# Batch 0's softmax with the maximum as exponential bias, and the preparation of w_in moved off GpSimd

## The chip, the cores and the metric

One core of one Trainium2 chip runs the whole program. The metric is device time in microseconds of one execution, as the median over runs; lower is better.

## What is computed

Three layers follow one another. Inputs are B=4 batches, H=8 heads, S=576 positions, head size 64 (so 2304 tokens of 512 features).

```python
scores = scale * q @ k.T                      # per batch and head
# heads 0-3: key at most 31 behind the query; heads 4-7: key behind, same position mod 32
scores = where(mask, scores, -1e9); scores -= scores.max(-1)
attn = exp(scores); attn /= attn.sum(-1) + 1e-9
x = (attn @ v), tokens by 512
h = x @ w_in                                  # 512 -> 1024, w_in is float64
sm = softmax(h); solu = h * sm; ln = layernorm(solu) * g_ln
x = ln @ w_out                                # 1024 -> 512, w_out is float64
logits = x @ w_gate + modality_bias[modality_id]; e = argmax(logits)
out = gate * (relu(x @ w1[e]) @ w2[e])        # 8 experts
```

## The kernel before

**Stages.** Attention runs in units. A unit is one group of query tiles of one head of a head pair: three tiles of 96 queries by 128 keys for the local heads, four tiles of 72 by 72 for the strided heads. A head pair has 4 units, a batch has 4 pairs, so 16 units: in batch 0 the two strided pairs come first (8 strided units), then the two local pairs (8 local units). `scores` (L310 to L350) makes a unit's matmuls (L326, TensorE to PSUM), adds the mask and takes the row maximum in one VectorE instruction for each tile (L333), and then forms the exponentials in one of two ways, chosen for each batch and head kind by the string `SHIFT_ON`. With "P" or "D", GpSimd or VectorE subtracts the maximum from all tiles of the unit in one instruction (L339), ScalarE takes one exponential over the unit (L342), and `normalise` sums it on VectorE (L357). With "0", VectorE makes the scaled negative maximum (L345, four numbers wide at most), ScalarE takes one exponential for each tile with it as bias and gives the row sum itself (L348, each followed by a read of the accumulator), and L357 is not issued. Before, batch 3 alone has "0". In both ways `normalise` then adds 1e-9 (L358), takes the reciprocal (L359) and multiplies, on GpSimd in most batches (L365). TensorE transposes the result (L127), ScalarE copies it out of PSUM (L376), TensorE multiplies by v (L385), and ScalarE and VectorE split the result into a high and a low part (L397, L398). Units overlap: a unit's transposes and its product with v come two units after its scores (`LAG = 2`).

**w_in.** The matrix multiplies work on float32 in a high and a low part. w_in comes as float64, in 8 pieces of 128 by 512, at fixed places among batch 0's attention steps (`W_IN_AT`). For a piece, `f64_piece` (L200) loads the raw words with SyncE's DMA queue (L203; three buffers, so a load waits for the last reader of the piece three before), scales the upper word (ScalarE L209 or GpSimd L211, by `MAG_ON`), puts in the sign, and ors in the low bits on VectorE (L220). By `SIGN_ON` the sign takes either one GpSimd multiplication by zero (L213) and one VectorE instruction (L214), or two VectorE instructions (L217, L218). `prep_w_in` then casts the high part on ScalarE (L228) and subtracts it for the low part on GpSimd (L229). The first 8 letters of `MAG_ON` and `SIGN_ON` are w_in's, the last 8 are w_out's, whose pieces follow in the same way (L231).

**Order.** The program text interleaves the stages step by step; the framework's scheduler orders the instructions of each engine from dependencies and from a simulated timeline. Each engine then runs its own list in order and waits on semaphores. The second layer (tile by tile of 128 tokens, matmuls L477 and L533) starts when batch 0's units are done; the attention of batches 1 to 3 and the preparation of w_out are spread between its steps by a written list (`TAKES`, `W_OUT_AT`). The experts come last.

Of the kernel before, what the change touches and what calls it, by code (L numbers as in the profile page):

```python
# [9 lines left out]
F32 = mybir.dt.float32  # L10
# [4 lines left out]
ALU = mybir.AluOpType  # L15
# [13 lines left out]
def tile_attention_moe_moe2(  # L29
# [15 lines left out]
    nc = tc.nc  # L45
# [23 lines left out]
    STAGES = "ATPV"  # L69
    PAIRS = [[2, 3, 0, 1]] + [[0, 1, 2, 3]] * (B - 1)  # L70
    NORM_ON = "PPPDPPPP"
    SHIFT_ON = "DPPPPP00"
    MAG_ON = "APAAPAAAPPPAAPPA"
    SIGN_ON = "PDDDDDPPDDDDDDDP"
    LOW_ON = "DPDDPDDD"
    W_IN_AT = [3, 5, 8, 26, 35, 39, 52, 66]
    W_OUT_AT = [1, 1, 2, 3, 3, 3, 4, 6]
# [17 lines left out]
    winH = cst.tile([P, KD, FF], F32R, name="winH")  # L95
    winL = cst.tile([P, KD, FF], F32R, name="winL")
# [104 lines left out]
    def f64_piece(src, tm, tw, by_act, sgn="D"):  # L201
        raw = rawp.tile([P, 512, 2], I32, name="raw")
        nc.sync.dma_start(raw, src)  # L203
        hi, lo = raw[:, :, 1], raw[:, :, 0]
        mag = mp.tile([P, 512], F32, name="mag", tag=tm)
        w = mp.tile([P, 512], F32, name="wf", tag=tw)
        wi = w.bitcast(I32)
        if by_act:
            nc.scalar.activation(mag, hi.bitcast(F32), AF.Copy, scale=REBIAS)  # L209
        else:  # L210
            nc.gpsimd.tensor_tensor(mag, hi.bitcast(F32), rebias.to_broadcast([P, 512]), ALU.mult)  # L211
        if sgn == "P":
            nc.gpsimd.tensor_tensor(hi.bitcast(F32), hi.bitcast(F32), zeros.to_broadcast([P, 512]), ALU.mult)  # L213
            nc.vector.scalar_tensor_tensor(  # L214
                wi, mag.bitcast(I32), 3, hi, ALU.logical_shift_left, ALU.bitwise_or)
        else:
            nc.vector.tensor_scalar(wi, mag.bitcast(I32), 3, None, ALU.logical_shift_left)  # L217
            nc.vector.scalar_tensor_tensor(  # L218
                wi, hi, -2147483648, wi, ALU.bitwise_and, ALU.bitwise_or)
        nc.vector.scalar_tensor_tensor(  # L220
            wi, lo, 29, wi, ALU.logical_shift_right, ALU.bitwise_or)
        return w

    def prep_w_in(i):
        c, hf = divmod(i, 2)
        cs = slice(hf * 512, hf * 512 + 512)
        w = f64_piece(w_in32[:, c, cs], "e", "so", MAG_ON[i] == "A", SIGN_ON[i])
        nc.scalar.copy(winH[:, c, cs], w)  # L228
        nc.gpsimd.tensor_tensor(winL[:, c, cs], w, winH[:, c, cs].bitcast(F32), ALU.subtract)  # L229

    def prep_w_out(f):  # L231
        w = f64_piece(w_out32[:, f], "nH", "yt", MAG_ON[8 + f] == "A", SIGN_ON[8 + f])
        g = gln[:, f:f + 1]
        dst = ((slice(0, HALF), slice(0, HALF)), (slice(HALF, DM), slice(YA, YA + HALF)))
        pool = LOW_ON[f] == "P"
        if pool:
            nc.scalar.activation(w, w, AF.Copy, scale=g)
            g = 1.0
        for s_, d_ in dst:
            nc.scalar.activation(woH[:, f, d_], w[:, s_], AF.Copy, scale=g)  # L240
        for s_, d_ in dst:
            if pool:
                nc.gpsimd.tensor_tensor(woL[:, f, d_], w[:, s_], woH[:, f, d_].bitcast(F32), ALU.subtract)
            else:
                nc.vector.scalar_tensor_tensor(
                    woL[:, f, d_], w[:, s_], g, woH[:, f, d_].bitcast(F32), ALU.mult, ALU.subtract)
        return f, w, g
# [64 lines left out]
    def scores(b, hp, tiles, j, qT, kT):  # L312
# [18 lines left out]
        for i, t in enumerate(tiles):  # L331
# [3 lines left out]
                mx[:nq, i:i + 1])  # L335
        xb = SHIFT_ON[2 * b + (not local)]
        if xb != "0":
# [294 lines left out]
    for i, at_ in enumerate(W_IN_AT):  # L632
        take(at_)
        prep_w_in(i)
# [623 lines left out]
```

## Time and profile before

| | |
|---|---|
| median of 3 runs | 667.8 us (667.05 to 668.77) |
| the profiled execution | 673.7 us, of which its span 672.0 us |
| TensorE busy (matmul) | 614.2 us, 91% of the span |
| VectorE busy | 373.6 us, 56% |
| ScalarE busy | 317.2 us, 47% |
| GpSimd busy | 190.9 us, 28% |

PE is TensorE, PEld its weight loads, DVE VectorE, ACT ScalarE, POOL GpSimd, SP SyncE. A group is all instructions of one line, engine, operation and shape; a wait is idle time of an engine just before an instruction, with what ended it. An engine's busy time includes time in which one of its instructions had started and stood still. The granted clock is a share of TensorE's full 2.4 GHz, so 0.5 is its lower level, 1.2 GHz.

### The profile page before, as it was taken

Reading aid. Unit: us, or ns where it says so; the run is one execution under the profiler, and the core shown is the slowest. Engines: PE = TensorE matmul, PEld = TensorE weight load, DVE = VectorE, ACT = ScalarE, POOL = GpSimd, SP = SyncE. Lnnn points to the kernel's source line nnn. Section 1 sums busy time; section 2 is a strip of 40 time slices with the busy share of each in tenths; the row PEclk is TensorE's granted clock in tenths of the full one; section 3 lists DMA queues with packets and bytes.
Section 4 is the critical chain, followed back from the end, with each engine's and each line's share of the span. In section 5 each row is a group of like instructions: output and inputs, shape, how many; then the busy total and the mean of one; then the engine's idle time right before and its main releaser. Section 6 shows DMA issues by size and latency. Waiting matters only on the chain. (4 is left out here: it accounts for less than half of the span.)

```text
span 672.0 us, 12841 instructions
## 1 busy us (share of the span) xinstructions
PE 614.2 (91%) x4536; PEld 552.3 (82%) x4536; DVE 373.6 (56%) x1367; ACT 317.2 (47%) x723; POOL 190.9 (28%) x243
## 2 busy tenths in 40 slices
PE   5648798999999999998999999999899898999993
PEld 4546687899998989887988999889788787898892
DVE  2999688867776765566569663224346452211120
ACT  3556666746765567778537442223435343221220
POOL 4876344411343234121100422320120302112011
PEclk9555697999999999999999999999899999999997
DMA  8656322121311221111034020253527362112010
GB/s 217 150 152 166 93 72 81 36 66 56 97 52 54 69 74 42 35 34 35 18 131 150 32 90 25 65 177 121 195 82 249 100 213 93 32 64 63 17 48 23
DMA packets 54774, 60.00 MB, mean 89 GB/s; under 512 B 39313, under 2 KB 39313, under 8 KB 54675
## 3 DMA queue, kind: packets, MB, share of 16 engines
q1 hardware_dynamic: 47810, 42.52, 22.2%
q0 software_dynamic: 4272, 11.57, 5.5%
q10 hardware_dynamic: 2592, 4.72, 1.9%
q8 instruction: 47, 0.77, 0.5%
q14 instruction: 53, 0.43, 0.2%
HBM read 49.05 MB, written 10.26 MB: 88 GB/s over the span
## 5 line engine op out<-in xcount | busy, mean ns | idle before, releaser
L845 PE MATMUL py<-w2H,winL 128*128 128x512 f32 x288 | 92.0, 395 | 0.0
L885 PE MATMUL pf<-xTH,w1H 128*128 128x256 f32 x288 | 82.5, 287 | 3.7 <-DVE yo L984 3.7
L885 PE MATMUL pf<-xTL,w1H 128*128 128x256 f32 x288 | 81.5, 283 | 0.3 <-DVE xTL L824 0.3
L885 PE MATMUL pf<-xTH,w1L 128*128 128x256 f32 x288 | 81.4, 283 | 0.0
L892 DVE SCALAR_TENSOR_TENSOR winL<-pf,winL 128x512 fp32r<-128x512 f32 x36 | 24.9, 692 | 95.7 <-ACT winL L891 95.6
L326 PE MATMUL S<-kz,qT 128*72 128x72 f32 (+1 forms) x448 | 60.1, 283 | 17.5 <-DVE mx L333 8.9
L326 PEld LDWEIGHTS S<-kz,qT 128*72 128x72 f32 (+1 forms) x448 | 51.6, 179 | 22.4 <-ACT kz L310 10.5
L365 POOL TENSOR_TENSOR ex<-ex,rd 96x384 f32<-96x384 f32 (+1 forms) x56 | 45.3, 811 | 76.2 <-DVE rd L359 58.3
L891 ACT ACTIVATE winL<-pf 128x512 fp32r<-128x512 f32 x36 | 21.6, 599 | 88.0 <-PE pf L885 87.3
L845 PEld LDWEIGHTS py<-w2H,winL 128*128 128x128 f32 x288 | 53.4, 188 | 10.5
L885 PEld LDWEIGHTS pf<-xTH,w1H 128*128 128x128 f32 x288 | 56.2, 195 | 5.6 <-issue 2.5
L477 PE MATMUL ph<-winH,xTH 128*128 128x512 f32 x144 | 59.9, 416 | 0.1
L477 PE MATMUL ph<-winL,xTH 128*128 128x512 f32 x144 | 57.8, 402 | 0.0
L477 PE MATMUL ph<-winH,xTL 128*128 128x512 f32 x144 | 57.4, 404 | 0.0
L885 PEld LDWEIGHTS pf<-xTL,w1H 128*128 128x128 f32 x288 | 56.2, 195 | 0.8 <-DVE xTL L824 0.5
L885 PEld LDWEIGHTS pf<-xTH,w1L 128*128 128x128 f32 x288 | 56.2, 195 | 0.0
L851 POOL DMA_INDIRECT out_dram<-yo,idx x14 | 14.1, 1007 | 144.3 <-ACT yo L850 121.4
L339 POOL TENSOR_TENSOR ex<-ex,mx 72x288 f32<-72x288 f32 (+1 forms) x40 | 31.3, 784 | 76.7 <-DVE mx L333 42.3
L533 PE MATMUL pa<-woH,nL 128*128 128x264 f32 x144 | 42.8, 297 | 0.0
L533 PE MATMUL pa<-woH,nH 128*128 128x264 f32 x144 | 41.8, 290 | 0.3 <-ACT nH L522 0.3
L533 PE MATMUL pb<-woH,nL 128*128 128x256 f32 x144 | 41.4, 287 | 0.0
L533 PE MATMUL pa<-woL,nH 128*128 128x264 f32 x144 | 41.0, 285 | 0.0
(244 smaller groups left out, 1637.0 us busy)
## 6 DMA issues: line engine op xcount, KB each, us to landing
raw<-in_moe_w_dram SPq DMA_DIRECT2D x36, 512.0 KB
y_d<-yt ACTq DMA_DIRECT2D x18, 256.0 KB
raw<-in_moe_w_in_dram SPq DMA_DIRECT2D x8, 512.0 KB
raw<-in_moe_w_out_dram SPq DMA_DIRECT2D x8, 512.0 KB
vn<-in_v_dram SPq DMA_DIRECT2D x16, 160.0 KB
qn<-in_q_dram SPq DMA_DIRECT2D x8, 288.0 KB
kn<-in_k_dram SPq DMA_DIRECT2D x8, 288.0 KB
vn<-in_v_dram SPq DMA_DIRECT2D x8, 288.0 KB
```

The costliest lines, as they stand in the source:

```text
L326: nc.tensor.matmul(sp_[:nq, i, :nk], qT[:, q0:q0 + nq], kT[:, half, k0:k0 + nk], start=True, stop=True)
L339: eng.tensor_tensor(ex[:nq, :nt, :nk], ex[:nq, :nt, :nk], mx[:nq, :nt].unsqueeze(2).to_broadcast([nq, nt, nk]), ALU.subtract)
L365: nc.gpsimd.tensor_tensor(ex[:nq, :nt, :nk], ex[:nq, :nt, :nk], rd[:nq, :nt].unsqueeze(2).to_broadcast([nq, nt, nk]), ALU.mult)
L477: nc.tensor.matmul(ph, a[:, c, ts_], w[:, c, cs], start=n == 0, stop=n == 3 * KD - 1)
L533: nc.tensor.matmul(p, a[:, f], w[:, f, cols], start=n == 0, stop=n == 3 * KF - 1)
L845: nc.tensor.matmul(p, a[:, f, s], x, start=n == 0, stop=n == 3 * KF - 1)
L851: nc.gpsimd.indirect_dma_start(out=out[:, :], out_offset=indirect(idx[:, col, 2:3].bitcast(U32)), in_=o, in_offset=None, bounds_check=NT - ...
L885: mm = nc.tensor.matmul(p[:, u], a[:, c, fs], x[:, c], start=n == 0, stop=n == 3 * KD - 1)
L891: last[0] = (nc.scalar.activation(hH[:, f2s], p, AF.Relu), nc.vector.scalar_tensor_tensor(hL[:, f2s], p, 0.0, hH[:, f2s].bitcast(F32), ALU ...
L892: nc.vector.scalar_tensor_tensor(hL[:, f2s], p, 0.0, hH[:, f2s].bitcast(F32), ALU.max, ALU.subtract))
```

## The change

Batch 0's two letters of `SHIFT_ON` become "0" (they were VectorE for the local heads and GpSimd for the strided ones). All of w_in's scalings go to ScalarE (pieces 1 and 4 were on GpSimd), all its sign steps to VectorE's two instructions (pieces 0, 6 and 7 used GpSimd), and all 8 subtractions for the low part to VectorE. w_out's letters stay.

```diff
-    SHIFT_ON = "DPPPPP00"
-    MAG_ON = "APAAPAAAPPPAAPPA"
-    SIGN_ON = "PDDDDDPPDDDDDDDP"
+    SHIFT_ON = "00PPPP00"
+    MAG_ON = "AAAAAAAAPPPAAPPA"
+    SIGN_ON = "DDDDDDDDDDDDDDDP"
...
         nc.scalar.copy(winH[:, c, cs], w)
-        nc.gpsimd.tensor_tensor(winL[:, c, cs], w, winH[:, c, cs].bitcast(F32), ALU.subtract)
+        nc.vector.tensor_tensor(winL[:, c, cs], w, winH[:, c, cs].bitcast(F32), ALU.subtract)
```

## Rows read from the trace of the kernel before

**Rows 1.** Busy time by engine in stretches: span, PE, PEld, DVE, ACT, POOL, clock, DMA share, GB/s.

```profile
13.00:74.00 61.00, 36.88 (x258) 30.68 (x260) 56.88 (x185) 35.43 (x71) 42.66 (x45) 0.58 0.61 156
74.00:135.00 61.00, 56.57 (x371) 48.98 (x368) 47.71 (x170) 39.35 (x94) 27.27 (x32) 0.86 0.24 64
135.00:480.00 345.00, 336.85 (x2722) 307.07 (x2720) 210.05 (x919) 185.38 (x459) 81.91 (x107) 1.00 0.25 76
```

**Rows 2.** Groups of VectorE, 0 to 75 us: count | busy us, mean ns | idle before.

```profile
L218 DVE SCALAR_TENSOR_TENSOR wf<-raw,wf 128x512 int32<-128x512 int32 x7 | 7.7, 1107 | 0.1
L214 DVE SCALAR_TENSOR_TENSOR wf<-mag,raw 128x512 int32<-128x512 int32 x3 | 7.2, 2387 | 3.0 <-POOL raw L213 3.0
L339 DVE TENSOR_TENSOR ex<-ex,mx 96x384 f32<-96x384 f32 x8 | 6.7, 834 | 0.0
...
L358 DVE TENSOR_SCALAR rd<-den 72x4 f32<-72x4 f32 x8 | 4.7, 594 | 0.0
...
L357 DVE TENSOR_REDUCE den<-ex 72x4 f32<-72x288 f32 x8 | 3.4, 430 | 0.0
L357 DVE TENSOR_REDUCE den<-ex 96x3 f32<-96x384 f32 x6 | 3.2, 531 | 0.0
```

**Rows 3.** Two lines over the whole span: duration ns min/median/max, first and last start.

```profile
L220 DVE SCALAR_TENSOR_TENSOR wf<-raw,wf x16: 671/679/1928, 17.1 to 129.4; 128x512 int32<-128x512 int32 x16
...
L345 DVE TENSOR_SCALAR nb<-mx x16: 155/163/261, 252.7 to 320.6; 96x3 f32<-96x3 f32 x8, 72x4 f32<-72x4 f32 x8
```

**Rows 4.** Timeline near 45 us, VectorE, then GpSimd: start us, length us.

```profile
44.79 4.35 DVE L214 SCALAR_TENSOR_TENSOR wf<-mag,raw 128x512 int32<-128x512 int32 x1
...
45.09 1.28 POOL L365 TENSOR_TENSOR ex<-ex,rd 72x288 f32<-72x288 f32 x2
...
47.56 1.03 POOL L213 TENSOR_TENSOR raw<-raw,zeros 128x512 f32<-128x512 f32 x1
```

**Rows 5.** Groups of GpSimd and of ScalarE, 0 to 75 us.

```profile
L229 POOL TENSOR_TENSOR winL<-wf,winH 128x512 fp32r<-128x512 f32 x8 | 11.2, 1406 | 2.1 <-ACT winH L228 2.1
...
L339 POOL TENSOR_TENSOR ex<-ex,mx 72x288 f32<-72x288 f32 x8 | 6.6, 831 | 2.0 <-DVE mx L333 1.7 <-DVE rd L359 0.3
...
L213 POOL TENSOR_TENSOR raw<-raw,zeros 128x512 f32<-128x512 f32 x3 | 3.1, 1036 | 7.3 <-ACT mag L209 7.3
...
L209 ACT ACTIVATE mag<-raw 128x512 f32<-128x512 f32 x7 | 4.7, 669 | 4.3 <-DMA raw<-in_moe_w_in_dram 3.1 <-DVE wf L214 1.1
```

**Rows 6.** ScalarE's waits, 13 to 74 us: total us, times, longest us.

```profile
ACT winH L228 <- DVE wf L220: 9.1, 6, 4.2
ACT ex L342 <- POOL ex L339: 3.5, 3, 2.1
...
ACT ex L342 <- DVE rd L358: 2.1, 1, 2.1
ACT ex L342 <- DVE ex L339: 1.8, 1, 1.8
```

**Rows 7.** Timeline of ScalarE around exponentials of both ways: start us, length us.

```profile
41.33 0.44 ACT L342 ACTIVATE ex<-ex 72x288 f32<-72x288 f32 x1
41.67 0.65 ACT L310 COPY kz<-ptq 64x288 f32<-64x288 f32 x1
...
53.10 0.53 ACT L342 ACTIVATE ex<-ex 96x384 f32<-96x384 f32 x1
53.53 0.39 ACT L376 COPY pT<-pP 72x288 f32<-72x288 f32 x1
...
253.53 0.42 ACT L348 ACTIVATE ex<-ex,nb 96x128 f32<-96x128 f32 x1
...
253.93 0.40 ACT L348 ACTIVATE ex<-ex,nb 96x128 f32<-96x128 f32 x1
...
311.89 0.36 ACT L348 ACTIVATE ex<-ex,nb 72x72 f32<-72x72 f32 x1
...
313.26 0.38 ACT L376 COPY pT<-pP 72x288 f32<-72x288 f32 x1
```

## The prediction, made before the changed kernel ran

> **What bounds the kernel now.** Read the busy times by stretch first, since the shares over the whole span mix stages. Everything that the change touches lies ahead of 74 us: batch 0's attention and the preparation of w_in. In the stretch from 13 us (where the first piece of w_in reaches ScalarE) to 74 us, VectorE is busy 56.9 of 61.0 us, 93%, while TensorE has 36.9 us at a granted clock of 0.58 [rows 1]. Behind it TensorE leads: 56.6 of 61 us up to 135 us, 336.9 of 345 us up to 480 us [rows 1]. So the front is set by VectorE, and since the second layer cannot start before batch 0's units are done, what the front saves or costs moves all that follows. The chain that ended last can't be used here, because it runs through the experts and not back to the front.
>
> Then read what VectorE does in those 57 us. Much of it is standing still. The same kind of instruction, 128 by 512 with two inputs in SBUF, takes 0.68 us at the median [rows 3], but the three of L214 average 2.39 us and the seven of L218 1.11 us, and L358 on four numbers takes 0.59 us [rows 2] where an instruction of the same size and kind takes 0.16 [rows 3]. The timeline shows one case: a 4.35 us L214 from 44.79 us, while GpSimd runs four instructions end to end from 45.09 to 48.59 us; VectorE's ends half a microsecond after GpSimd's last [rows 4]. The sums over a unit, L357, stay at 0.43 and 0.53 us [rows 2]. VectorE loses time to GpSimd, and GpSimd is busy 42.7 us of the stretch [rows 1].
>
> **The change part by part.**
>
> *VectorE.* Gone: 8 subtractions (L339, 6.7 us), the sums (L357, 3.4 and 3.2 us in the window), three L214 (7.2 us): 20.5 us [rows 2]. Added: 16 small L345 at 0.16, 2.6 us [rows 3]; for three pieces one L217 and one L218, six instructions taken at 0.68 each, 4.1 us; 8 subtractions of w_in's low part. These have no VectorE row; the nearest is L220, of the same shape with two SBUF inputs, 0.68 us [rows 3], so 5.4 us; the low end is L220's smallest, 0.67, the high end GpSimd's own 1.41 us [rows 5], 11.2 us. Net 12.1 - 20.5 = -8.4 us. What stays and waited: L358 lost 8 x (0.59 - 0.16) = 3.4 us, L218 lost 7 x (1.11 - 0.68) = 3.0 us. GpSimd loses L229, its L339 and L213, 11.2 + 6.6 + 3.1 = 20.9 us [rows 5], and two scalings, which is half its load in the front; I let half of the 6.4 us go. VectorE: 56.9 - 8.4 - 3.2 = 45.3 us, between 42.1 (no waits left) and 54.3 (waits whole, subtractions at 1.41).
>
> *ScalarE.* The price of an exponential is the distance from its start to the next start, since neighbours overlap. Before: 41.67 - 41.33 = 0.34 us for a strided unit, 53.53 - 53.10 = 0.43 for a local one. The other way is seen in batch 3: four tiles of 72 by 72 take 313.26 - 311.89 = 1.37 us, one of 96 by 128 takes 0.40, three 1.2 us [rows 7]. So 8 x (1.37 - 0.34) + 8 x (1.20 - 0.43) = 8.2 + 6.2 = 14.4 us, and two scalings at 0.67 [rows 5] make 15.7 us. ScalarE: 35.4 + 15.7 = 51.1 us. It becomes the fullest engine of the front. The Trainium skill, "ScalarE: Activation LUTs", section "Step-by-step: what each stage is for", gives one element per cycle and lane whatever the function; by that alone cutting an exponential into tiles costs nothing, ScalarE would stand near 36.8 us and VectorE would go on to set the front. The rows disagree: three pieces cost 1.20 us where the whole cost 0.43, so the sum goes by the rows.
>
> *ScalarE's waits.* It is idle 61.0 - 35.4 = 25.6 us. Of that go the waits of L342 for subtractions and for what stood in front of them, 3.5 + 2.1 + 1.8 = 7.4 us [rows 6], and the scaling's 1.1 us for L214 [rows 5]. The 9.1 us for L220 [rows 6] shrink, because the chain of a piece on VectorE was stretched by GpSimd (the 4.35 us above); I keep a third, 3.0. That leaves 25.6 - 8.5 - 6.1 = 11.0 us if nothing else moves. An engine with more in its queue covers part of its remaining waits (they run out while it works): I take half, 5.5 us, between 0 and 11.0. The front then lasts 51.1 + 5.5 = 56.6 us in place of 61.0: 4.4 us less; from 9.9 less to 1.1 more at the ends.
>
> *Queues.* No DMA is added or moved in the text, but SyncE's loads of w_in wait for L220, the last reader of a buffer, so they start earlier as the pieces finish earlier; with a DMA share of 0.61 in the front [rows 1] there is room. In front of ScalarE's queue stand two more scalings that wait for a load, and behind them copies and exponentials that TensorE and VectorE wait for: part of the 11.0 us end. GpSimd falls to about 22 us of the front and is nowhere near a bound; that VectorE's new subtractions make it wait is covered by this room. The new small L345 sits between maximum and exponential, and replaces a subtraction of 0.83 us in that place, so a unit's own chain gets longer by about 0.3 us at most (1.37 + 0.16 against 0.83 + 0.34 for a strided unit); this is hidden while two units overlap, and costs 16 x 0.3 = 4.8 us if they don't, which the high end holds.
>
> *Sum.* The profiled execution took 673.7 us with a span of 672.0, that is 5.9 us above the median of 667.8; I carry the difference over. 667.8 - 4.4 = **663.4 us**.
>
> **The rivals.**
>
> *All of VectorE's relief counts.* ScalarE covers all its waits, and the front is 51.1 us long: 667.8 - 9.9 = 657.9. For it: at the start VectorE also sat idle 3.0 us for GpSimd's L213 [rows 2], which is gone, and VectorE itself kept 93% busy in the front. Against: ScalarE depends on TensorE and VectorE several times in each unit. The rule of the skill's page on elements per cycle would also end near here, since VectorE's 45.3 us would leave some 10 us. Chance 0.17.
>
> *No change.* The front ends earlier, but the stretch from 74 to 135 us takes the gain back: there the clock is 0.86, so TensorE loses time to it, and VectorE is at 47.7 of 61 us [rows 1]; or VectorE's waits do not fall as GpSimd empties, because its new subtractions compete with GpSimd too, and it stays near 54 us. 667.8. Against: nothing in that stretch is tied to absolute time, and its DMA share is 0.24. Chance 0.17.
>
> *Slower: ScalarE's in-order queue becomes the front.* The place is L228, which waits for L220 at ScalarE's head of queue while exponentials and PSUM copies stand behind it. If those 9.1 us stay whole, since VectorE now has the subtractions of the low part between two pieces, and half of the other 8.0 us is covered, ScalarE needs 51.1 + 9.1 + 4.0 = 64.2 us, 3.2 more than now: 671.0. It decides from an idle time of 61.0 - 51.1 = 9.9 us upward. For it: 15.7 us of work go to a serial engine, which is more than the 8.5 us of waits that certainly go. Against: the long L220 waits coincide with VectorE's stalls behind GpSimd. Chance 0.19.
>
> **How the numbers follow.** A measurement of this kernel can tell about 0.3%, 2 us, from no change. The forecast, some 4 us less, has 0.47; with the first rival, faster has 0.64; same 0.17; slower 0.19. The range goes from 656 (the first rival's 657.9, and part of the 3.0 us at the start) to 671 (the slower rival). The likeliest cases have one sign, between 657.9 and 665.8.
>
> **What would show it.** In the changed profile: L348 in the front, 56 more of them; L214 there no longer; L358 near 0.3 us on the mean; VectorE near 45 us in the front and ScalarE near 51, now the fuller; the last maximum of batch 0 and the first matmul of the second layer (L477) some 4 us earlier; the stretch behind about as long as now. The forecast is wrong if ScalarE's idle time for L220 stays near 9 us, if VectorE's own instructions still average well over 0.7 us for 128 by 512, or if the front shortens and the stretch to 135 us grows by as much.

## The result, and the profile after

The changed kernel takes 663.85 us (median of 20 runs, 658.7 to 669.48), the kernel before 670.19 us in the runs beside them (20 runs, 667.05 to 673.55). The ratio is 0.9899 with a 95% interval of 0.9876 to 0.9923: 6.8 us or 1.0% faster, where 4.4 us were forecast. The ratio leaves out three slow runs of the changed kernel that its median of 20 holds, which is why the two medians differ by 6.3 us only. With more runs the median of before has moved up from 667.8 us; so the forecast of 663.4 us comes so close to the measured time because a smaller gain was taken from a lower start; the gain is the number to judge it by. The profiled execution took 667.01 us with a span of 665.3 us, 6.7 us less than that of before.

First the first two stretches of [rows 1], of the changed kernel (columns as there):

```profile
13.00:74.00 61.00, 37.61 (x301) 31.16 (x302) 46.51 (x206) 54.08 (x180) 23.62 (x31) 0.80 0.66 167
74.00:135.00 61.00, 55.34 (x404) 49.00 (x402) 48.12 (x180) 37.27 (x91) 23.27 (x28) 0.94 0.22 58
```

In the front VectorE fell from 56.88 to 46.51 us, ScalarE rose from 35.43 to 54.08 us, and GpSimd fell from 42.66 to 23.62 us. ScalarE is now the fullest engine there. Since the front is shorter, part of these 61 us is work that used to come later.

The groups of VectorE, 0 to 75 us, that answer to [rows 2]:

```profile
L220 DVE SCALAR_TENSOR_TENSOR wf<-raw,wf 128x512 int32<-128x512 int32 x10 | 8.1, 806 | 0.0
L218 DVE SCALAR_TENSOR_TENSOR wf<-raw,wf 128x512 int32<-128x512 int32 x10 | 6.8, 684 | 0.0
...
L229 DVE TENSOR_TENSOR winL<-wf,winH 128x512 fp32r<-128x512 f32 x8 | 5.6, 698 | 1.9 <-ACT winH L228 1.9
...
L358 DVE TENSOR_SCALAR rd<-den 72x4 f32<-72x4 f32 x8 | 1.9, 240 | 0.0
L345 DVE TENSOR_SCALAR nb<-mx 72x4 f32<-72x4 f32 x8 | 1.4, 179 | 0.0
```

L214 is gone, L218 has come down from 1107 to 684 ns, L358 on four numbers from 594 to 240 ns. The new subtraction L229 takes 698 ns, hardly more than the 679 ns of L220's median [rows 3].

ScalarE's groups of the same stretch, and its waits from 13 to 74 us, beside [rows 5, 6]:

```profile
L348 ACT ACTIVATE ex<-ex,nb 72x72 f32<-72x72 f32 x32 | 11.0, 347 | 0.2
L348 ACT ACTIVATE ex<-ex,nb 96x128 f32<-96x128 f32 x24 | 9.4, 391 | 3.3 <-DVE nb L345 3.1 <-DVE rd L359 0.2
...
L228 ACT CAST winH<-wf 128x512 fp32r<-128x512 f32 x8 | 4.9, 618 | 0.0
```

```profile
ACT mag L209 <- DMA raw<-in_moe_w_in_dram: 5.1, 3, 3.2
ACT ex L348 <- DVE nb L345: 3.1, 2, 2.1
```

The 9.1 us in which L228 waited for L220 are gone altogether. What is left is 5.1 us for the loads of w_in (3.1 us before, [rows 5]), which ScalarE reaches before they have landed, and 3.1 us for the small L345.

The timeline shows the price of the split exponentials and where the second wait comes from (start us, length us):

```profile
24.11 0.35 ACT L348 ACTIVATE ex<-ex,nb 72x72 f32<-72x72 f32 x1
...
25.48 0.60 ACT L228 CAST winH<-wf 128x512 fp32r<-128x512 f32 x1
...
44.01 0.08 DVE L333 DVE_READ_ACCUMULATOR2_ANT mx<- 96x1 f32 x1
44.01 0.42 DVE L217 TENSOR_SCALAR wf<-mag 128x512 int32<-128x512 int32 x1
...
44.35 0.68 DVE L229 TENSOR_TENSOR winL<-wf,winH 128x512 fp32r<-128x512 f32 x1
44.95 0.16 DVE L345 TENSOR_SCALAR nb<-mx 96x3 f32<-96x3 f32 x1
...
45.20 0.40 ACT L348 ACTIVATE ex<-ex,nb 96x128 f32<-96x128 f32 x1 [0.94 <-DVE nb L345]
...
45.60 0.39 ACT L348 ACTIVATE ex<-ex,nb 96x128 f32<-96x128 f32 x1
```

Four strided exponentials take 25.48 - 24.11 = 1.37 us, and a local one 0.40 us from start to start. Both are what [rows 7] gave. The maximum is complete at 44.09 us, but two instructions of w_in's preparation stand ahead of L345 in VectorE's list, and ScalarE sits idle 0.94 us for them.

The second layer's first matmul shows what reached TensorE (L477, 60 to 80 us: duration ns min/median/max, first and last start); before, then after:

```profile
L477 PE MATMUL ph<-winH,xTH x2: 775/775/775, 72.0 to 75.2; 128*128 128x512 f32 x2
```

```profile
L477 PE MATMUL ph<-winH,xTH x8: 389/396/499, 66.3 to 78.6; 128*128 128x512 f32 x8
```

It starts 5.7 us earlier. The same matmul takes 0.40 us where it took 0.78: before, the granted clock is 0.50, the lower level, from 72 to 76 us, and after it is 1.00, the upper level, from 68 to 92 us. The first output tile of the second layer (L538) leaves PSUM at 135.88 instead of 143.44 us, 7.6 us earlier; the tenth at 288.59 instead of 295.79 us, 7.2 us earlier; the span ends 6.7 us earlier.

The first L477 is not the end of batch 0's attention, though the description of the kernel and the prediction take it so. L477 adds up the four head pairs, and its first matmuls need the first local pair only. In the changed kernel the exponentials of two of the eight local units start behind it, at 66.44 and 69.27 us; before, at 74.75 and 75.87 us. The first instruction that needs a sum over all four pairs is L481, the row maximum of half an output tile: 87.29 us before, 77.93 us after, 9.4 us earlier.

### The profile page after: what moved, and what is told of

It reads as the page before. It is cut to its first block, busy times and chain, and to the rows that moved or that the text cites. A ratio compares the mean times of both kernels' runs of the same rounds, so it can differ in the third digit from the quotient of the medians.

```text
span 665.3 us, 12941 instructions
## 1 busy us (share of the span) xinstructions
PE 609.3 (92%) x4536; PEld 548.2 (82%) x4536; DVE 359.1 (54%) x1370; ACT 330.6 (50%) x821; POOL 166.4 (25%) x222
## 5 line engine op out<-in xcount | busy, mean ns | idle before, releaser
L365 POOL TENSOR_TENSOR ex<-ex,rd 96x384 f32<-96x384 f32 (+1 forms) x56 | 44.5, 795 | 101.1 <-DVE rd L359 68.9
L326 PE MATMUL S<-kz,qT 128*72 128x72 f32 (+1 forms) x448 | 57.9, 276 | 7.5 <-DVE mx L333 4.1
L477 PE MATMUL ph<-winH,xTH 128*128 128x512 f32 x144 | 59.7, 415 | 3.1 <-DVE so L492 2.0
L326 PEld LDWEIGHTS S<-kz,qT 128*72 128x72 f32 (+1 forms) x448 | 50.2, 175 | 11.1 <-DVE mx L333 5.3
L477 PE MATMUL ph<-winL,xTH 128*128 128x512 f32 x144 | 57.6, 400 | 0.0
L477 PE MATMUL ph<-winH,xTL 128*128 128x512 f32 x144 | 57.1, 401 | 0.0
L348 ACT ACTIVATE ex<-ex,nb 72x72 f32<-72x72 f32 (+1 forms) x112 | 40.7, 368 | 9.3 <-DVE nb L345 8.4
L339 POOL TENSOR_TENSOR ex<-ex,mx 96x384 f32<-96x384 f32 (+1 forms) x32 | 24.6, 770 | 78.5 <-DVE mx L333 47.5
```

What stands on the lines that cost most here:

```text
L326: nc.tensor.matmul(sp_[:nq, i, :nk], qT[:, q0:q0 + nq], kT[:, half, k0:k0 + nk], start=True, stop=True)
L339: eng.tensor_tensor(ex[:nq, :nt, :nk], ex[:nq, :nt, :nk], mx[:nq, :nt].unsqueeze(2).to_broadcast([nq, nt, nk]), ALU.subtract)
L348: nc.scalar.activation(ex[:nq, i, :nk], ex[:nq, i, :nk], AF.Exp, bias=nb[:nq, i:i + 1], scale=SCALE, accum_out=den[:nq, i:i + 1])
L365: nc.gpsimd.tensor_tensor(ex[:nq, :nt, :nk], ex[:nq, :nt, :nk], rd[:nq, :nt].unsqueeze(2).to_broadcast([nq, nt, nk]), ALU.mult)
L477: nc.tensor.matmul(ph, a[:, c, ts_], w[:, c, cs], start=n == 0, stop=n == 3 * KD - 1)
```

## The experiments

The experiments were timed in five rounds beside the kernel before, whose median was 669.4 to 671.0 us there. "First L477", "first L481" and "first L538" are start times in the one profiled execution of each kernel (in e4, e5 and e6 added lines move the numbers by 3, 1 and 2); the ratio is to the kernel before in the same rounds.

| kernel | median us | ratio (95%) | first L477 | first L481 | first L538 | span |
|---|---|---|---|---|---|---|
| before | 670.19 | 1 | 71.99 | 87.29 | 143.44 | 672.0 |
| after | 663.85 | 0.9899 (0.9876 to 0.9923) | 66.29 | 77.93 | 135.88 | 665.3 |
| e1 shift alone | 669.66 | 0.998 (0.9947 to 1.0013) | 67.48 | 80.25 | 138.45 | 671.0 |
| e2 w_in alone | 663.63 | 0.986 (0.9818 to 0.9903) | 68.95 | 79.93 | 133.71 | 661.6 |
| e3 low part back on GpSimd | 668.84 | 0.996 (0.9931 to 0.9988) | 66.69 | 80.95 | 140.73 | 667.9 |
| e4 one exponential | 659.11 | 0.9811 (0.9775 to 0.9847) | 62.66 | 74.25 | 129.46 | 656.9 |
| e5 extra GpSimd reads | 676.65 | 1.0085 (1.0056 to 1.0114) | 66.74 | 79.22 | 136.87 | 675.5 |
| e6 extra GpSimd memsets | 672.42 | 1.0028 (1.0001 to 1.0054) | 62.09 | 76.37 | 132.84 | 669.5 |
| e7 local shift on GpSimd | 664.4 | 0.9898 (0.986 to 0.9936) | 65.47 | 76.47 | 132.08 | 662.3 |
| e8 strided shift on GpSimd | 660.86 | 0.9844 (0.9806 to 0.9881) | 62.48 | 78.61 | 132.70 | 659.5 |
| e9 reads, late order kept | 673.01 | 1.0056 (1.0029 to 1.0083) | 69.64 | 83.23 | 144.25 | 671.6 |
| e10 memsets, late order kept | 665.2 | 0.9929 (0.99 to 0.9957) | 65.13 | 76.82 | 134.49 | 661.1 |
| e11 low part alone | 670.85 | 1.0014 (0.9986 to 1.0041) | 65.38 | 80.90 | 139.82 | 668.1 |
| e12 sign and scaling alone | 663.25 | 0.99 (0.9869 to 0.9932) | 67.40 | 79.82 | 136.18 | 662.0 |

### The change in two halves: e1 and e2

e1 is the kernel before with the new exponentials alone:

```diff
-    SHIFT_ON = "DPPPPP00"
+    SHIFT_ON = "00PPPP00"
```

> Only batch 0's exponentials per tile; w_in stays as before. Theory A (VectorE stood still behind GpSimd, and emptying GpSimd is what counts): VectorE loses 12 us of work, but w_in's GpSimd work (L229, L213, two L211, some 17 us) still holds it, and ScalarE's waits for L220 stay near 9 us; a gain of 1 to 3 us against before. Theory B (VectorE's own work was the bound, and handing subtraction and sums to ScalarE is what counts): nearly the whole gain, 5 us or more. Slower than before would say that ScalarE's longer queue costs more than it frees.

Measured: 0.998, no difference that can be told. Its VectorE groups, 0 to 75 us, then its ScalarE waits, 13 to 66 us:

```profile
L358 DVE TENSOR_SCALAR rd<-den 72x4 f32<-72x4 f32 x8 | 5.9, 742 | 3.0 <-ACT ex L348 3.0
L214 DVE SCALAR_TENSOR_TENSOR wf<-mag,raw 128x512 int32<-128x512 int32 x3 | 5.0, 1665 | 2.8 <-POOL raw L213 2.8
```

```profile
ACT ex L348 <- DVE nb L345: 5.1, 3, 2.3
...
ACT winH L228 <- DVE wf L220: 0.4, 1, 0.4
```

VectorE's long instructions are all still there, L358 even longer than before. L228's wait for L220 is gone although w_in's preparation is as before, so that wait was no mark of w_in's part: ScalarE, with more in its queue, comes to L228 later.

e2 is the other half:

```diff
-    MAG_ON = "APAAPAAAPPPAAPPA"
-    SIGN_ON = "PDDDDDPPDDDDDDDP"
+    MAG_ON = "AAAAAAAAPPPAAPPA"
+    SIGN_ON = "DDDDDDDDDDDDDDDP"
...
-        nc.gpsimd.tensor_tensor(winL[:, c, cs], w, winH[:, c, cs].bitcast(F32), ALU.subtract)
+        nc.vector.tensor_tensor(winL[:, c, cs], w, winH[:, c, cs].bitcast(F32), ALU.subtract)
```

> Only w_in's part of the change; batch 0's exponentials as before. Theory A: VectorE gets about 2 us more work on paper, but GpSimd loses 17 us in the front and VectorE's stretched instructions shrink (L218 from 1.1 to below 0.8 us, L358 from 0.6 to below 0.4); a gain of 3 to 5 us. Theory B: no gain or a loss, since VectorE stays the fullest engine with more work (0 to 3 us slower).

Measured: 0.986, a gain of some 9 us where 3 to 5 were expected, and no less than the whole change. Of its VectorE groups, 0 to 75 us:

```profile
L229 DVE TENSOR_TENSOR winL<-wf,winH 128x512 fp32r<-128x512 f32 x8 | 5.9, 738 | 0.0
...
L358 DVE TENSOR_SCALAR rd<-den 72x4 f32<-72x4 f32 x8 | 2.4, 296 | 0.0
```

GpSimd still subtracts for the strided units, yet L358 is down to 296 ns. By the time, the gain is w_in's, and the exponentials add nothing that can be told. By the first L481 it is not: there e1 is 7.0 us ahead of the kernel before and e2 7.4 us. e1 loses its lead behind that point.

### The parts of w_in: e3, e11 and e12

e3 is the changed kernel with the subtraction of the low part back on GpSimd (the last pair of lines above, reversed). e11 is the kernel before with only that subtraction on VectorE. e12 is the kernel before with only `MAG_ON` and `SIGN_ON` changed.

> The changed kernel with w_in's eight low-part subtractions back on GpSimd (11 us for GpSimd, 5.6 us off VectorE). Theory A: VectorE's stretched instructions return (L218, L220 and L358 together 3 us or more above the changed kernel), and 2 to 4 us of the 6 us gain are lost. Theory B: nothing is lost, since VectorE has less to do: as fast as the changed kernel or faster.

> One line of the change alone: w_in's eight low-part subtractions on VectorE, all letters as before. VectorE gets 5.6 us more of its own work, GpSimd loses 11.2. If what GpSimd does costs VectorE more than its own work: 3 to 6 us faster than before, most of what w_in's part gave (9 us). If it is the sign and scale steps that count: within 2 us of before.

> The other two thirds of w_in's part alone: all scalings on ScalarE, all signs on VectorE, the low part left on GpSimd. GpSimd loses 5.8 us, VectorE's three L214 (7.2 us, stretched) become L217 and L218. If it is the amount of GpSimd work in the front that counts: 2 to 4 us faster than before, less than the low part alone. If the long single stops count (L214 of 4.35 us): as much as the low part alone or more.

Measured: 0.996, 1.0014 and 0.990. Scalings and signs alone bring as much as the whole change. The low part is worth 0.6% on top of the rest of the change (0.9899 against 0.996) and nothing alone: e11 missed its 3 to 6 us. The parts don't add up.

Nor do VectorE's stops order these times. Of e12's VectorE groups, 0 to 75 us:

```profile
L220 DVE SCALAR_TENSOR_TENSOR wf<-raw,wf 128x512 int32<-128x512 int32 x10 | 10.4, 1035 | 0.0
...
L358 DVE TENSOR_SCALAR rd<-den 72x4 f32<-72x4 f32 x8 | 5.0, 626 | 0.0
```

GpSimd is busy 47.5 us of these 75 in e12 (48.4 before), L220 and L358 take longer than before (859 and 594 ns there), L218 still 772 ns and only L214 is gone, yet e12 is as fast as the whole change. In e11 GpSimd has nearly as much, 46.9 us, but L220 is down to 723 ns, L358 to 236 and the three L214 to 1162 on the mean, and nothing is gained. So freeing VectorE is not by itself what makes the time shorter. The first L481 is much the same in e1, e2, e3, e11 and e12, 79.8 to 81.0 us, 6.3 to 7.5 us earlier than before, while the times differ by 1.5%: what separates these kernels lies behind that point.

In e11's profile the front is 6.6 us shorter by the first L477, and the first L538 only 3.6 us earlier. One wait of TensorE between the two is as long as the loss (waits of e11, 66 to 140 us):

```profile
PE ph L477 <- DVE so L492: 3.0, 1, 3.0
```

L492 frees the PSUM tile that the next L477 fills. What stands ahead of it in VectorE's list is seen in its timeline, 108 to 120 us, in e11 and then at the same step in e2, where this wait is 0.7 us:

```profile
116.11 0.55 DVE L357 TENSOR_REDUCE den<-ex 96x3 f32<-96x384 f32 x1 [1.58 <-ACT ex L342]
...
116.72 0.68 DVE L481 TENSOR_REDUCE hmx<-ph 128x1 f32<-128x512 f32 x1
...
119.13 0.87 DVE L214 SCALAR_TENSOR_TENSOR wf<-mag,raw 128x512 int32<-128x512 int32 x1
119.92 0.67 DVE L492 SCALAR_TENSOR_TENSOR so<-e,ph 128x512 f32<-128x512 f32 x1
```

```profile
112.28 0.68 DVE L481 TENSOR_REDUCE hmx<-ph 128x1 f32<-128x512 f32 x1
...
114.86 0.68 DVE L492 SCALAR_TENSOR_TENSOR so<-e,ph 128x512 f32<-128x512 f32 x1
```

The instructions are the same, their order is not. In e11, L481 stands behind a sum that waits 1.58 us for ScalarE, and L214, a step of a piece of w_out, stands just ahead of L492: 119.92 - 116.72 = 3.2 us from L481 to L492, against 2.58 us in e2, and the 1.58 us ahead of that. The scheduler rewrites these lists for the whole program when the front changes. TensorE waits 3.0 us for L492 in e1, e3, e9 and e11, the kernels with the least gain of those whose late order is kept, and 2.0 us in the changed kernel, 0.7 us in e2, 0.5 us in e12. That this order costs them the gain fits the numbers; a kernel with only the order changed was not tried, so it is not shown.

A second thing separates the same kernels, the granted clock from 74 to 135 us: 0.86 before and in e9, 0.88 in e3, 0.90 in e1 and e11, against 0.94 in the changed kernel, e7, e10 and e12 and 0.96 to 0.97 in e2, e4 and e8. By an estimate from these figures, 0.86 is 17 us of the 61 at the lower level and 0.94 is 7; at the lower level L477 takes 0.78 us in place of 0.40, so the 10 us between them are worth some 5 us of TensorE's work, most of the gain. The two come together: behind its 3.0 us wait e11's next L477 takes 0.79 us and the clock is 0.57 from 120 to 124 us, while behind the wait of 0.7 us e2's takes 0.50 us and the clock stays at 1.00. No run separates the order, the wait and the clock, so how much of the gain each is worth stays open.

### Is ScalarE the front's bound now: e4, e7 and e8

e4 leaves the subtraction of the maximum out in batch 0, takes one exponential for each unit, and sums on VectorE. e7 and e8 go back to GpSimd's subtraction for the local and for the strided units of batch 0; both compute everything.

```diff
-    SHIFT_ON = "00PPPP00"
+    SHIFT_ON = "NNPPPP00"
...
+        if xb == "N":
+            nc.scalar.activation(ex[:nq, :nt, :nk], ex[:nq, :nt, :nk], AF.Exp, scale=SCALE)
+            return ex, nq, nk, None
```

```diff
-    SHIFT_ON = "00PPPP00"
+    SHIFT_ON = "P0PPPP00"
```

```diff
-    SHIFT_ON = "00PPPP00"
+    SHIFT_ON = "0PPPPP00"
```

> The changed kernel with one exponential for each unit of batch 0 and no maximum subtracted there (left out: that subtraction; the sums go back to VectorE, L357). ScalarE loses 14 us in the front, VectorE gains about 4. If ScalarE sets the changed kernel's front (theory A's end state), another 3 to 6 us are gained, the first L477 comes near 62 us, and VectorE is the fuller again. If the front is set by loads or by the units' own chains, the time stays at the changed kernel's within 2 us.

> The changed kernel with batch 0's local units shifted by GpSimd as batches 1 and 2 are (8 subtractions of 0.8 us on GpSimd, one exponential a unit, sums on VectorE). ScalarE loses about 6 us in the front, VectorE gains about 3, GpSimd 6.6. If ScalarE sets the front, 2 to 4 us faster than the changed kernel; if VectorE's waits for GpSimd matter more, as fast or slower.

> The changed kernel with batch 0's strided units shifted by GpSimd as before. ScalarE loses about 8 us between 13 and 40 us, VectorE gains about 2, GpSimd 6.6. If ScalarE sets the front there, 2 to 4 us faster than the changed kernel; if the loads of the first 30 us set it, the same time.

Measured: 0.9811, 0.9898 and 0.9844. The engines from 13 to 62 us (columns as in [rows 1]), in the changed kernel, then e4, then e8:

```profile
13.00:62.00 49.00, 27.81 (x220) 23.53 (x221) 42.33 (x176) 42.48 (x143) 19.84 (x25) 0.79 0.75 189
```

```profile
13.00:62.00 49.00, 32.71 (x255) 27.80 (x257) 45.11 (x180) 33.66 (x69) 25.05 (x24) 0.90 0.67 179
```

```profile
13.00:62.00 49.00, 31.39 (x243) 26.61 (x243) 44.01 (x183) 36.31 (x94) 31.91 (x31) 0.93 0.74 189
```

With ScalarE relieved by 8.8 us, e4 begins the second layer 3.6 us earlier than the changed kernel and is 0.9% faster than it, with intervals that don't touch, though VectorE does more. So ScalarE's queue is part of what sets the front now, or the units' own chain, which loses L345 in e4 as well. e8 relieves it by 6.2 us at the cost of 12 us of GpSimd, and its median is 3 us lower; the two intervals just touch, at 0.988. e7 relieves it by 3.9 us (38.57 us in that stretch) and gains nothing. By the ratio e8 and e2 are the two fastest of the kernels that compute everything. That it matters which units have their maximum as bias is not shown, since the intervals of e7 and e8 overlap.

### What holds VectorE: e5, e6, e9 and e10

Each adds to the changed kernel useless GpSimd work behind pieces of w_in, into a buffer that is not yet in use. e5 reads two tiles of SBUF and writes one, once for each piece; e6 only writes, three times for each:

```diff
+        nc.gpsimd.tensor_tensor(csum[:, 0:512], w, winH[:, c, cs].bitcast(F32), ALU.subtract)
```

```diff
+        for _ in range(3):
+            nc.gpsimd.memset(csum[:, 0:512], 0.0)
```

> The changed kernel with eight useless GpSimd subtractions added, one behind each piece of w_in, of the same shape as those that the change took away (about 11 us of GpSimd in the front, results never read). If VectorE stands still behind GpSimd instructions that read SBUF, its two-input instructions stretch again (L218, L220, L229 and L358 together 3 us or more above the changed kernel) and the time goes up by 1 to 4 us, though nobody waits for the added work. If only the work on VectorE and the dependencies count, nothing changes.

> The control of the run before: in place of each added subtraction three GpSimd memsets of 128 by 512, which only write (about 11 us in all). If it is reading that counts, VectorE's two-input instructions stay near 0.68 us and the time stays at the changed kernel's; if any GpSimd work counts, the stretch and the loss are those of the run before.

Measured: 1.0085 and 1.0028, both slower, the memsets too, though e6 has the earliest first L477 of all. In e5 the stops came as expected (L229 1090 ns and L359, elsewhere L358, 563 ns on the mean, against 698 and 240 in the changed kernel), but neither time is a measure of the front, for most of the loss lies 300 us behind it. TensorE's waits of e5, 300 to 400 us, and GpSimd's timeline there; then GpSimd's timeline of the changed kernel:

```profile
PE pa L534 <- DVE LG L541: 6.2, 1, 6.2
```

```profile
356.62 0.96 POOL L508 TENSOR_TENSOR rstd<-rstd,mhalf 128x1 f32<-128x1 f32 x1
...
383.70 0.58 POOL L508 TENSOR_TENSOR rstd<-rstd,mhalf 128x1 f32<-128x1 f32 x1
```

```profile
367.70 0.57 POOL L507 TENSOR_TENSOR rstd<-rstd,mhalf 128x1 f32<-128x1 f32 x1
...
374.10 0.57 POOL L507 TENSOR_TENSOR rstd<-rstd,mhalf 128x1 f32<-128x1 f32 x1
```

L507 (L508 with the added line) makes the layer norm's factor, for which the output tile waits. The changed kernel puts one after every second table store of GpSimd, 6.4 us apart; e5's list has five stores and four gathers between two of them, 27.1 us. e6 shows the same wait with 5.8 us. The order came out differently because GpSimd's work in the front had changed.

e9 and e10 repeat the two with numbers of extra instructions for which GpSimd's order at that place is the one of the changed kernel: ten subtractions (two for each of the first five pieces) and 18 memsets (three for each of the first six).

> The run with added GpSimd subtractions again, so chosen (two behind each of the first five pieces, ten in all, about 13 us, results never read) that GpSimd's list behind 300 us keeps the order of the changed kernel, table stores and gathers behind the layer norm's powers. In the first two runs with added work that order had changed and TensorE waited 6 us there, so their times say little on the front. If VectorE stands still behind GpSimd's reads: L229 and L358 stretch as they did (1.1 and 0.6 us against 0.7 and 0.25), and the time is 2 to 5 us above the changed kernel's (ratio to before 0.992 to 0.998). If the loss of the first two runs was all of the late order: the changed kernel's time (0.990).

> The control again, with 18 memsets behind the first six pieces (about 10 us of GpSimd that only writes) and the late order kept as in the changed kernel. If only reading GpSimd work holds VectorE: ratio to before within 0.003 of the changed kernel's 0.990, L229 near 0.72 us. If any GpSimd work does: as the run with reads.

Measured: 1.0056 and 0.9929. The memsets cost 0.3% at most against the changed kernel, as expected; the subtractions cost 1.6%, more than expected. The timeline shows the cases of contact. GpSimd and then VectorE in e6, six memsets in a row:

```profile
18.01 3.72 POOL L231 MEMSET csum<- 128x512 f32 x6
...
18.16 0.68 DVE L218 SCALAR_TENSOR_TENSOR wf<-raw,wf 128x512 int32<-128x512 int32 x1
18.76 0.68 DVE L229 TENSOR_TENSOR winL<-wf,winH 128x512 fp32r<-128x512 f32 x1
19.43 0.68 DVE L220 SCALAR_TENSOR_TENSOR wf<-raw,wf 128x512 int32<-128x512 int32 x1
```

and in e9, where GpSimd reads:

```profile
17.88 4.55 POOL L229 TENSOR_TENSOR csum<-wf,winH 128x512 f32<-128x512 f32 x2
...
29.27 1.26 POOL L229 TENSOR_TENSOR csum<-wf,winH 128x512 f32<-128x512 f32 x1
30.50 1.11 POOL L365 TENSOR_TENSOR ex<-ex,rd 72x288 f32<-72x288 f32 x1
31.57 2.66 POOL L229 TENSOR_TENSOR csum<-wf,winH 128x512 f32<-128x512 f32 x2
...
18.00 0.68 DVE L218 SCALAR_TENSOR_TENSOR wf<-raw,wf 128x512 int32<-128x512 int32 x1
18.61 0.68 DVE L229 TENSOR_TENSOR winL<-wf,winH 128x512 fp32r<-128x512 f32 x1
...
19.28 0.68 DVE L220 SCALAR_TENSOR_TENSOR wf<-raw,wf 128x512 int32<-128x512 int32 x1
...
28.84 2.24 DVE L229 TENSOR_TENSOR winL<-wf,winH 128x512 fp32r<-128x512 f32 x1
31.00 2.11 DVE L217 TENSOR_SCALAR wf<-mag 128x512 int32<-128x512 int32 x1
33.15 1.64 DVE L218 SCALAR_TENSOR_TENSOR wf<-raw,wf 128x512 int32<-128x512 int32 x1
```

Beside memsets VectorE keeps its 0.68 us. Beside GpSimd's reads one of the two engines stands still, and not always the same one: from 17.88 us it is GpSimd, whose two subtractions take 4.55 us while VectorE keeps its 0.68; from 28.84 us it is VectorE, whose instructions of the same kinds take 2.24 and 1.64 us, and L217, which takes 0.42 us elsewhere, 2.11. The Trainium skill, "SBUF — State Buffer", section "Who interferes with whom", says that a VectorE instruction with two inputs in SBUF contends with a GpSimd instruction that reads SBUF and not with one that only writes it; both timelines agree. The comparison of the two times has a limit: most of e10's memsets run before 20.5 us, ahead of most of the front's VectorE work, and add 3 us to GpSimd there from 13 to 66 us, while the subtractions add 13 us and have the units' own L365 behind them. They also read a buffer that the next piece writes, for which VectorE waits 1.35 us once in e9. The timelines, not the times, are the evidence.

## Why the prediction was right, and where it was not

**The stops** were read rightly: VectorE stands still beside GpSimd's reads, and with w_in's work taken away (e2) most of the stops go; e9 brings them back. That VectorE's stops set the time is not shown: e12 keeps most of them and gains 1%, e11 loses more of them and gains nothing. e9's first L481 is 5.3 us later than the changed kernel's and its first L538 8.4 us later; what is lost between the two comes with the 3.0 us wait and the clock of 0.86.

**VectorE's sum** held: 11.6 us less were predicted (56.9 to 45.3), and up to the first L477 VectorE is busy 43.55 us from 13 us on, where it was 54.88, 11.3 us less. L229 was taken at 0.68 and took 0.698 us. The waits that were only half counted went almost whole: L218's 3.0 us are gone, L358 keeps 8 x 0.08 us of its 3.4; L220, which the sum left as it was, still averages 806 ns (859 before).

**ScalarE's price** held: by the timeline 1.37 and 0.40 us, as read from batch 3, and up to the first L477 e1 has 12.1 us more than before (45.55 against 33.44), with eight strided and six local units done, for which the forecast's prices give 8.2 + 4.6 = 12.8. The elements-per-cycle rule of the Trainium skill ("ScalarE: Activation LUTs", "Step-by-step: what each stage is for") is one for a filled pipe; taken alone, it would have made e1 free for ScalarE, and it was not. **Its idle time**, 5.5 us predicted, came out as 6.5 us from 13 us to the first L477, by other waits: the kept third of L228's wait (3.0 us) went to nothing, and the loads and L345 took its place. The prediction named both (two scalings that wait for a load, and the small L345 in a unit's chain), but priced neither in the likeliest case.

**The size** was too small: 4.4 us forecast, 6.8 measured (5.2 to 8.3 by the interval). The mis-sized terms are two. Up to the first L477 the front became 5.7 us shorter, since ScalarE's added work there was 13.3 us (46.8 against 33.4) and not 15.7, in part because two of the eight local units still come behind it; its waits fell by 19.0 us, where the forecast had 20.1. And the stretch from there to the first L538, which was to be "about as long as now", became 1.9 us shorter. The granted clock in the front rose from 0.58 to 0.80, which no step had; but e7 has 0.61 and e12 0.59 from 13 to 66 us with the same ratio as the changed kernel, so the front's clock is not needed for the gain. Nor does the clock of a whole execution go with its time: of the 70 runs of the kernel before in the rounds, the 27 with a mean clock of 0.962 or more average 670.8 us, and the other 43, all below 0.957, 670.5 us.

**What failed** is the step from the front to the time: "what the front saves or costs moves all that follows". e11 saves 6.6 us at the first L477 and nothing in the time, e6 9.9 us and is slower, e2 saves only 3.0 us and is as fast as the whole change. In part this is the wrong mark, for "the second layer cannot start before batch 0's units are done" does not hold; but at the first L481, too, e2's lead of 7.4 us grows to 9.7 us at the first L538 while e11's 6.4 us shrink to 3.6. The first L538 orders the kernels nearly as the ratios do (e5 and e6 aside, whose loss comes later), and the first L477 does not. The rival of no change was held down by the argument that "nothing in that stretch is tied to absolute time". It named the right place, and with the clock of 0.86 there one of the two things found in it; what it did not have is that the lists of VectorE and ScalarE there are written anew, and that TensorE's wait for L492 grows up to 3.0 us. In the changed kernel the wait is 2.0 us and the clock 0.94, and the gain held. That it held is in part luck, for nothing in the forecast told the changed kernel from e1, e3 or e11 in that stretch.

**The parts** were not told apart: the forecast credited the exponentials with the larger part of VectorE's relief and charged them with nearly all of ScalarE's 15.7 us. By e1 and e2 the change without the exponentials does no worse.

**The rival of a slower kernel** needed 9.1 us of waits for L220; none are left.

## What to carry to other kernels

Where a profile shows one engine's instructions of one shape at two durations, find what runs beside the long ones, and count what these stops cost before counting instructions. Judge a shorter front not by the moment when the next stage begins, which may need only part of the front, but by its first finished output, and look at the engines' order behind it, for a scheduler may rewrite lists hundreds of microseconds away. Undo each part of a combined change alone, and compare more than the time: here five kernels save 6 to 8 us by the first L481 and end 1.5% apart.

## What the runs showed that was not expected

A chain of GpSimd reads holds VectorE even on tiny or one-input instructions: L217 for 2.11 us in e9, L358 on four numbers for 742 ns on the mean in e1 against 149 in e4. GpSimd loses as well: its two subtractions in e9 from 17.88 us took 4.55 us, where one alone takes 1.26. No run here shows what decides which of the two loses. Eight useless instructions in the first 55 us came with a 6.2 us stop of TensorE that ends at 388 us, behind another order of GpSimd's list; in e9, with ten of them and the old order, TensorE is busy 98.26 of the 100 us from 300 us on, in e5 89.93.
